# Transposing Q and K as bf16 halves, and centring K by the full-sequence mean, in a grouped-query attention kernel

## The chip, the cores and the metric

The kernel runs on one core of a Trainium2 chip. The metric is device time in microseconds. One run is one execution. The kernel before takes 653.99 us (median of 12 runs, 653.10 to 654.54). Executions agree within about 0.3%, so a difference of 1% is well outside the noise, and one of 0.2% needs several runs of both kernels side by side.

## The reference

Sixteen batches, 16 query heads that share 8 key/value heads two by two, 384 queries, 384 keys, head size 256, all in bf16:

```python
B, Hq, Hkv, Sq, Sk, D = 16, 16, 8, 384, 384, 256
# q, k, v: normal * 0.05, bf16
k = jnp.repeat(k, rep, axis=1); v = jnp.repeat(v, rep, axis=1)      # rep = 2
scores = jnp.einsum("bhqd,bhkd->bhqk", q, k) * D ** -0.5
p = softmax(scores, axis=-1)
return jnp.einsum("bhqk,bhkd->bhqd", p, v)
```

Entries of 0.05 make the scaled scores about 0.0025 in size, so every row of the softmax is almost flat and the output is nearly the mean of V. Comparing outputs on these inputs therefore hardly tests the scores at all.

## The kernel before

The work is 128 groups, one per batch and key/value head. A group has 768 query rows (two heads) and 384 keys. TensorE does three things per group: it transposes Q and K so that the head dimension lies on the partitions, it multiplies them (scores, transposed, keys on partitions), and it multiplies the exponentials with V (PV). One extra column of ones in V yields the row sums. The stages of neighbouring groups are interleaved in thirds of a slot, so that TensorE always has something to do.

The head size is 256, twice the partition count. The kernel before reads each pair of bf16 numbers as one f32 word, so one f32 transpose moves both:

```python
qT_sb  = ... sbuf_tensor("qT_sb",  [P, NBT, NQ], F32)     # bf16 pairs, interleaved
kT_sb  = ... sbuf_tensor("kT_sb",  [P, NBK, Sk], F32)
kcT_sb = ... sbuf_tensor("kcT_sb", [P, NBT, Sk], F32)
...
# TensorE, T(g, part): three row blocks
for s, (kind, t) in enumerate(parts[part]):
    src = (q_sb if kind == "q" else k_sb)[:, sl, t, :].bitcast(F32)
    i = pe.transpose(tr_ps[bank][:, s * P:(s + 1) * P], src, ident[:])     # ident is f32
```

What arrives is interleaved: partition p holds dimensions 2p and 2p+1 of token 0, then of token 1, and so on. The score matmul therefore picks every second element of both operands, even ones first, odd ones second, and adds the two products:

```python
# TensorE, ST(g, c)
for e in range(2):
    i = pe.matmul(st_ps[bank][:, 0:CW],                                    # CW = 384
                  lhsT=kcb[:, 2 * j * P + e:2 * (j + 1) * P:2],            # stationary, stride 2
                  rhs=qTb[:, 2 * h * CW + e:2 * (h + 1) * CW:2],           # moving, stride 2
                  start=(e == 0), stop=(e == 1))
```

`lhsT` is the stationary operand (128x128; the trace records a weight load for each matmul, 97 ns in the scores), `rhs` the moving one (128x384 in the scores; the wider it is, the further apart the matmuls start: 55.8 ns at 128 bf16 columns and 162.5 ns at 384 in the changed kernel). Before that, K is centred: a mean over keys is subtracted from each dimension, which leaves the softmax unchanged. VectorE sums the first 128 keys (`NMEAN = P`), and POOL subtracts:

```python
# VectorE, KRED(g)
kTb = kT_sb[:, slk, 0:NMEAN].bitcast(BF16).rearrange("p (k e) -> p e k", e=2)
i = dve.tensor_reduce(out=nsum_sb[:, slk, :], in_=kTb, axis=AX.X, op=ALU.add, negate=True)
# POOL, ksub(g): kc = NMEAN * k - sum, for e in 0, 1
i = pool.tensor_scalar(out=kcb[:, e::2], in0=kTb[:, e::2], scalar1=float(NMEAN),
                       scalar2=nsum_sb[:, slk, e:e + 1], op0=ALU.mult, op1=ALU.add)
```

ACT copies the transposes out of PSUM, the memory that TensorE writes to (EV), and computes the exponentials (EXP); VectorE divides by the row sums (NORM).

The softmax here doesn't subtract the row's maximum and nothing guards it: scores larger than these inputs give would overflow.

## Time and profile before

| | before |
|---|---|
| time, median | 653.99 us |
| TensorE busy | 99% of the span |
| ACT, VectorE, POOL busy | 74%, 73%, 27% |
| period of one group (PV starts 92 groups apart, divided by 92) | 5.000 us |

First the profile's page of the kernel before: the busy time of each engine, and the chain of work that ended last, by engine and by line. (PE is TensorE, PEld its weight loads, DVE is VectorE, ACT is ScalarE, POOL is GpSimd, and SPq the queue that issues the transfers.)

```profile
PE 643.8 (99%) x4992; PEld 499.0 (77%) x4992; DVE 472.5 (73%) x1664; ACT 483.4 (74%) x1153; POOL 173.4 (27%) x263
...
PE 98%; DMA 1%; DVE 1%; SPq 0%; issue 0%
PE ps L228 40%; PE ps L245 39%; PE ps L213 19%; DMA q_sb<-in_q_dram 1%; DVE o_sb L348 0%; DVE rs_sb L345 0%; SPq L141 0%; SPq L136 0%
```

TensorE is busy 99% of the time, and following each instruction back to what released it stays on TensorE for 98% of the span. Line 228 is the score matmul, 245 PV, 213 the transposes. The other engines have slack.

Busy time alone would not prove a bound, because the recorded durations of matmuls overlap. The groups of the page show it (the columns are line, engine, operation, output and inputs, sizes and count, then busy us and mean ns of one, then idle us before them):

```profile
L228 PE MATMUL ps<-qT_sb,kcT_sb 128*128 128x384 bf16 x1536 | 324.1, 332 | 0.0
L245 PE MATMUL ps<-v_sb,pT_sb 128*128 128x257 bf16 x2304 | 315.4, 272 | 0.2
L189 POOL TENSOR_SCALAR kcT_sb<-kT_sb,nsum_sb 128x384 bf16<-128x384 bf16 x256 | 172.6, 701 | 462.3 <-DVE nsum_sb L333 462.3
L304 ACT COPY qT_sb<-ps 128x384 f32<-128x384 f32 x256 | 122.6, 479 | 105.1 <-PE ps L213 105.1
L213 PE MATMUL ps<-ident,q_sb 128*128 128x128 f32 x768 | 127.0, 275 | 1.0 <-DMA q_sb<-in_q_dram 0.9
L333 DVE TENSOR_REDUCE nsum_sb<-kT_sb 128x2 f32<-128x256 bf16 x128 | 53.8, 420 | 11.0 <-ACT kT_sb L304 10.1
```

1536 score matmuls of 332 ns each would be 510 us, yet they cover 324 us. The cost of a matmul is the distance from its start to the next start, so read the timeline. This is TensorE of the kernel before in a stretch of 1.8 us (start, length, engine, line, what, and how many are merged):

```profile
300.14 0.49 PE L213 MATMUL ps<-ident,q_sb 128*128 128x128 f32 x3
300.47 0.84 PE L228 MATMUL ps<-qT_sb,kcT_sb 128*128 128x384 bf16 x4
301.15 0.82 PE L245 MATMUL ps<-v_sb,pT_sb 128*128 128x257 bf16 x6
301.81 0.49 PE L213 MATMUL ps<-ident,q_sb 128*128 128x128 f32 x3
```

Subtract neighbouring starts: three transposes take 0.33 us, four score matmuls 0.68 us, six PV matmuls 0.66 us, then it repeats. Averaged over single starts between 100 and 600 us, the spacing is 109.2 ns for an f32 transpose, 170.4 ns for a score matmul and 109.6 ns for PV. A group has 9, 12 and 18 of them: 9 x 109.17 + 12 x 170.42 + 18 x 109.58 = 5000 ns, exactly the period. Nothing else is in it.

### The profile page before, as it was taken

The page shows a single profiled execution, that of the slowest core. Times are in us where ns is not written, and L with a number is a line of the kernel's source. Part 1 is how long each engine was busy: PE and PEld are TensorE (multiplying, and loading weights), DVE is VectorE, ACT ScalarE, POOL GpSimd, SP SyncE. Part 2 cuts the span into 40 slices and gives each one's busy share as a digit, 9 for nine tenths or more (in the row PEclk, how much of TensorE's full clock was granted, in tenths as well). Part 3 has the DMA queues.
Part 4 walks back from the last instruction along what each step waited for, and adds up shares of the span by engine and source line. Part 5 has one row for each costly group of instructions (what it writes and reads, how often), then busy time and mean ns, then how long its engine had stood idle before and what let it go on. Part 6 is the DMA issues. An engine that isn't in the chain of part 4 may idle for free.

```text
span 651.6 us, 15000 instructions
## 1 busy us (share of the span) xinstructions
PE 643.8 (99%) x4992; PEld 499.0 (77%) x4992; DVE 472.5 (73%) x1664; ACT 483.4 (74%) x1153; POOL 173.4 (27%) x263
## 2 busy tenths in 40 slices
PE   7999999999999999999999999999999999999997
PEld 5777777777777777777777777777777777777775
DVE  2777777777777777777777777777777777777777
ACT  6777777777777777777777777777777777777774
POOL 3222322232223222222222232223222322232220
PEclk9999999999999999999999999999999999999999
DMA  7677777777777777777777777877777777777763
GB/s 254 215 227 239 247 236 229 234 230 245 237 247 242 232 235 239 243 230 238 241 241 227 241 222 236 249 241 234 240 232 242 247 234 229 242 243 238 229 203 117
DMA packets 125291, 151.99 MB, mean 233 GB/s; under 512 B 10272, under 2 KB 108960, under 8 KB 125216
## 3 DMA queue, kind: packets, MB, share of 16 engines
q1 hardware_dynamic: 125216, 151.04, 73.3%
q8 instruction: 41, 0.67, 0.5%
q14 instruction: 34, 0.28, 0.1%
HBM read 100.66 MB, written 50.33 MB: 232 GB/s over the span
## 4 chain that ended last, share of the span: by engine, by line
PE 98%; DMA 1%; DVE 1%; SPq 0%; issue 0%
PE ps L228 40%; PE ps L245 39%; PE ps L213 19%; DMA q_sb<-in_q_dram 1%; DVE o_sb L348 0%; DVE rs_sb L345 0%; SPq L141 0%; SPq L136 0%
## 5 line engine op out<-in xcount | busy, mean ns | idle before, releaser
L348 DVE TENSOR_TENSOR o_sb<-ps,rs_sb 128x256 bf16<-128x256 f32 x768 | 325.7, 424 | 26.4
L282 ACT ACTIVATE pT_sb<-ps 128x384 bf16<-128x384 f32 x768 | 337.9, 498 | 2.5 <-PE ps L228 2.5
L228 PE MATMUL ps<-qT_sb,kcT_sb 128*128 128x384 bf16 x1536 | 324.1, 332 | 0.0
L245 PE MATMUL ps<-v_sb,pT_sb 128*128 128x257 bf16 x2304 | 315.4, 272 | 0.2
L189 POOL TENSOR_SCALAR kcT_sb<-kT_sb,nsum_sb 128x384 bf16<-128x384 bf16 x256 | 172.6, 701 | 462.3 <-DVE nsum_sb L333 462.3
L245 PEld LDWEIGHTS ps<-v_sb,pT_sb 128*128 128x128 bf16 x2304 | 222.2, 97 | 77.7 <-DVE o_sb L348 1.2
L345 DVE RECIPROCAL rs_sb<-ps 128x1 f32<-128x1 f32 x768 | 124.9, 163 | 139.5 <-PE ps L245 129.6
L304 ACT COPY qT_sb<-ps 128x384 f32<-128x384 f32 x256 | 122.6, 479 | 105.1 <-PE ps L213 105.1
L228 PEld LDWEIGHTS ps<-qT_sb,kcT_sb 128*128 128x128 bf16 x1536 | 149.4, 97 | 61.1 <-issue 0.3
L213 PE MATMUL ps<-ident,q_sb 128*128 128x128 f32 x768 | 127.0, 275 | 1.0 <-DMA q_sb<-in_q_dram 0.9
L304 ACT COPY kT_sb<-ps 128x384 f32<-128x384 f32 x128 | 61.2, 478 | 53.5 <-PE ps L213 53.5
L213 PEld LDWEIGHTS ps<-ident,q_sb 128*128 128x128 f32 x768 | 93.0, 143 | 5.1 <-DMA q_sb<-in_q_dram 1.3
L213 PE MATMUL ps<-ident,k_sb 128*128 128x128 f32 x384 | 63.6, 275 | 3.4 <-DMA k_sb<-in_k_dram 3.4
L333 DVE TENSOR_REDUCE nsum_sb<-kT_sb 128x2 f32<-128x256 bf16 x128 | 53.8, 420 | 11.0 <-ACT kT_sb L304 10.1
L213 PEld LDWEIGHTS ps<-ident,k_sb 128*128 128x128 f32 x384 | 46.5, 143 | 5.1 <-issue 3.4
L304 ACT ACT_TABLE_LOAD x1 | 1.3, 1283 | 0.8 <-PEq L381 0.8
L174 POOL TENSOR_SCALAR_AFFINE_SELECT ident<-ones_sb 128x128 f32<-128x128 f32 x1 | 0.3, 292 | 0.1
L171 POOL MEMSET ones_sb<- 128x128 f32 x1 | 0.2, 204 | 0.3 <-POOLq L381 0.3
L381 POOL MEMSET const-float32-0.0<- 128x1 f32 x1 | 0.1, 98 | 0.3 <-issue 0.3
L177 POOL MEMSET v_sb<- 128x9 bf16 x1 | 0.1, 136 | 0.0
L381 POOL MEMSET const-bfloat16-1.0<- 128x1 bf16 x1 | 0.1, 102 | 0.0
L381 POOL MEMSET const-uint8-127<- 128x1 uint8 x1 | 0.1, 102 | 0.0
(1 smaller groups left out, 0.1 us busy)
## 6 DMA issues: line engine op xcount, KB each, us to landing
q_sb<-in_q_dram SPq DMA_DIRECT2D x256, 192.0 KB, 3.6
out_dram<-o_sb SPq DMA_DIRECT2D x127, 384.0 KB, 3.1
k_sb<-in_k_dram SPq DMA_DIRECT2D x128, 192.0 KB, 3.4
v_sb<-in_v_dram SPq DMA_DIRECT2D x128, 192.0 KB, 3.7
out_dram<-o_sb SPq DMA_DIRECT2D x3, 128.0 KB, 1.7
```

Of the source, the lines that this page charges most:

```text
L171: i = pool.memset(ones_sb[:], 1.0)
L174: pool.affine_select(out=ident[:], in_=ones_sb[:], pattern=[[-1, P]], compare_op=ALU.is_equal, fill=0.0, base=0, channel_multiplier=1)
L189: i = pool.tensor_scalar(out=kcb[:, e::2], in0=kTb[:, e::2], scalar1=float(NMEAN), scalar2=nsum_sb[:, slk, e:e + 1], op0=ALU.mult, op1=ALU ...
L213: i = pe.transpose(tr_ps[bank][:, s * P:(s + 1) * P], src, ident[:])
L228: i = pe.matmul(st_ps[bank][:, 0:CW], lhsT=kcb[:, 2 * j * P + e:2 * (j + 1) * P:2], rhs=qTb[:, 2 * h * CW + e:2 * (h + 1) * CW:2], start=( ...
L245: i = pe.matmul(o_ps[bank][:, 0:D + 1], lhsT=pT_sb[:, slp, j, t * P:(t + 1) * P], rhs=v_sb[:, slv, j, 0:D + 1], start=(j == 0), stop=(j == ...
L282: i = act.activation(out=pT_sb[:, slp, j, h * CW:(h + 1) * CW], in_=st_ps[bank][:, 0:CW], func=ACTF.Exp, bias=-C0, scale=scale / NMEAN)
L304: i = act.copy(out=dst, in_=tr_ps[bank][:, 0:nb * P])
L333: i = dve.tensor_reduce(out=nsum_sb[:, slk, :], in_=kTb, axis=AX.X, op=ALU.add, negate=True)
L345: i = dve.reciprocal(rs_sb[:, ri:ri + 1], o_ps[bank][:, D:D + 1])
L348: i = dve.tensor_tensor(out=o_sb[:, so, t, :], in0=o_ps[bank][:, 0:D], in1=rs_sb[:, ri:ri + 1].broadcast_to([P, D]), op=ALU.mult)
L381: nc = _bacc.Bacc("TRN2", target_bir_lowering=False, num_devices=1)
```

## The change

The change has two intentions: to transpose bf16 as bf16, in two halves of 128 dimensions, so that every operand is contiguous; and to centre K by the mean over all 384 keys. The core of the diff (helper functions, semaphore allocation and a constant that cancels in the softmax are cut):

```diff
-    NMEAN = P
+    NMEAN = Sk
-        qT_sb = ... [P, NBT, NQ], F32        kT_sb, kcT_sb likewise, ident F32
+        qT_sb = ... [P, NBT, 2, NQ], BF16    kT_sb, kcT_sb likewise, ident BF16
+        ksum_sb = es.enter_context(nc.sbuf_tensor("ksum_sb", [P, NBK, 2, P], F32))
 # TensorE, transposes
-                    src = (q_sb if kind == "q" else k_sb)[:, sl, t, :].bitcast(F32)
-                    i = pe.transpose(tr_ps[bank][:, s * P:(s + 1) * P], src, ident[:])
+                    src = q_sb if kind == "q" else k_sb
+                    for m in range(2):
+                        blk = m * nb + s
+                        i = pe.transpose(trb[:, blk * P:(blk + 1) * P],
+                                         src[:, sl, t, m * P:(m + 1) * P], ident[:])
 # TensorE, scores
-                                  lhsT=kcb[:, 2 * j * P + e:2 * (j + 1) * P:2],
-                                  rhs=qTb[:, 2 * h * CW + e:2 * (h + 1) * CW:2],
+                                  lhsT=kcT_sb[:, sl, m, j * P:(j + 1) * P],
+                                  rhs=qT_sb[:, sl, m, h * CW:(h + 1) * CW],
 # POOL
+            def kfold(g):      # 384 keys folded to 128 by two adds, waits for K's copy
+                ...
             for i in slots:
+                if valid(i + 2):
+                    ksub(i + 2)
                 if valid(i + 3):
-                    ksub(i + 3)
+                    kfold(i + 3)
 # VectorE
-                    if u == 0 and valid(i + 3):
-                        KRED(i + 3)          # summed kT_sb, first 128 keys
+                if valid(i + 3):
+                    KRED(i + 3)              # sums ksum_sb, at the end of the slot
```

ACT still copies the same bytes out of PSUM as 384 f32 words. One part of the diff shown matters for the schedule: the subtraction for a group now runs one slot later than before (a slot is one period of the interleaved stages).

More of the change, by code (lines that the diff above doesn't have):

```diff
@@ L13, with __init__ @@
 class Sem:
-    def __init__(self, nc, name):
-        self.h = nc.alloc_semaphore(name)
+    def __init__(self, es, nc, name):
+        self.h = es.enter_context(nc.semaphore(name))
         self.count = 0
@@ L32, in wait, with _split3 @@
         self.waited[key] = val
+def _split3(n):
+    base, rem = divmod(n, 3)
+    out_, s0 = [], 0
+    for x in range(3):
+        sz = base + (1 if x < rem else 0)
+        out_.append(list(range(s0, s0 + sz)))
+        s0 += sz
+    return out_
 def bass_standalone__gqa_softmax__near_ridge_kernel(nc, q, k, v, out):
@@ L42, in bass_standalone__gqa_softmax__near_ridge_kernel @@
     KT = Sk // P
-    DP = D // 2
-    assert DP == P and NQ % P == 0 and Sk % P == 0
+    assert D == 2 * P and NQ % P == 0 and Sk % P == 0 and Hq % Hkv == 0
     G = B * Hkv
     scale = float(D) ** -0.5
-    C0 = 50.0
+    C0 = 64.0
     VW = D + 8
-    CW = max(w for w in range(P, 513, P) if NQ % w == 0 and (NQ // w) * KT >= 1)
+    CW = max(w for w in range(P, 513, P) if NQ % w == 0)
     NCQ = NQ // CW
@@ L70, in bass_standalone__gqa_softmax__near_ridge_kernel @@
         v_sb = es.enter_context(nc.sbuf_tensor("v_sb", [P, NBV, KT, VW], BF16))
-        qT_sb = es.enter_context(nc.sbuf_tensor("qT_sb", [P, NBT, NQ], F32))
-        kT_sb = es.enter_context(nc.sbuf_tensor("kT_sb", [P, NBK, Sk], F32))
-        kcT_sb = es.enter_context(nc.sbuf_tensor("kcT_sb", [P, NBT, Sk], F32))
+        qT_sb = es.enter_context(nc.sbuf_tensor("qT_sb", [P, NBT, 2, NQ], BF16))
+        kT_sb = es.enter_context(nc.sbuf_tensor("kT_sb", [P, NBK, 2, Sk], BF16))
+        kcT_sb = es.enter_context(nc.sbuf_tensor("kcT_sb", [P, NBT, 2, Sk], BF16))
         pT_sb = es.enter_context(nc.sbuf_tensor("pT_sb", [P, NBP, KT, NQ], BF16))
         o_sb = es.enter_context(nc.sbuf_tensor("o_sb", [P, NBO, QT, D], BF16))
-        ident = es.enter_context(nc.sbuf_tensor("ident", [P, P], F32))
+        ident = es.enter_context(nc.sbuf_tensor("ident", [P, P], BF16))
         ones_sb = es.enter_context(nc.sbuf_tensor("ones_sb", [P, P], F32))
         nsum_sb = es.enter_context(nc.sbuf_tensor("nsum_sb", [P, NBK, 2], F32))
+        ksum_sb = es.enter_context(nc.sbuf_tensor("ksum_sb", [P, NBK, 2, P], F32))
         rs_sb = es.enter_context(nc.sbuf_tensor("rs_sb", [P, 16], F32))
         ps = es.enter_context(nc.psum_tensor("ps", [P, 8, 512], F32))
+        s_lk = [Sem(es, nc, f"lk{i}") for i in range(NBQ)]
+        s_lq = [[Sem(es, nc, f"lq{i}_{pp}") for pp in range(NPT)] for i in range(NBQ)]
+        s_lv = [Sem(es, nc, f"lv{i}") for i in range(NBV)]
+        s_so = [Sem(es, nc, f"so{i}") for i in range(NBO)]
+        s_tr = Sem(es, nc, "tr")
+        s_st = Sem(es, nc, "st")
+        s_pv = Sem(es, nc, "pv")
+        s_ex = Sem(es, nc, "ex")
+        s_ev = Sem(es, nc, "ev")
+        s_rc = Sem(es, nc, "rc")
+        s_nm = Sem(es, nc, "nm")
+        s_ns = Sem(es, nc, "ns")
+        s_cn = Sem(es, nc, "cn")
+        s_init = Sem(es, nc, "init")
+        s_pl = Sem(es, nc, "pl")
+        s_ks = Sem(es, nc, "ks")
         block = es.enter_context(nc.Block())
@@ L85, in bass_standalone__gqa_softmax__near_ridge_kernel @@
         o_ps = [ps[:, TRB + STB + b, :] for b in range(OB)]
-        s_lk = [Sem(nc, f"lk{i}") for i in range(NBQ)]
-        s_lq = [[Sem(nc, f"lq{i}_{pp}") for pp in range(NPT)] for i in range(NBQ)]
-        s_lv = [Sem(nc, f"lv{i}") for i in range(NBV)]
-        s_so = [Sem(nc, f"so{i}") for i in range(NBO)]
-        s_tr = Sem(nc, "tr")
-        s_st = Sem(nc, "st")
-        s_pv = Sem(nc, "pv")
-        s_ex = Sem(nc, "ex")
-        s_ev = Sem(nc, "ev")
-        s_rc = Sem(nc, "rc")
-        s_nm = Sem(nc, "nm")
-        s_ns = Sem(nc, "ns")
-        s_cn = Sem(nc, "cn")
-        s_init = Sem(nc, "init")
-        s_pl = Sem(nc, "pl")
         def grp(g):
@@ L128, in valid @@
             return 0 <= g < G
+        cs, ts, psl = _split3(NCH), _split3(QT), _split3(NPT)
         @block.sync
@@ L140, in load_qk @@
                     nb = len(parts[part])
-                    s_lq[sl][part].inc(sp.dma_start(q_sb[:, sl, t0:t0 + nb, :], qd[:, t0:t0 + nb, :]), 16)
+                    s_lq[sl][part].inc(
+                        sp.dma_start(q_sb[:, sl, t0:t0 + nb, :], qd[:, t0:t0 + nb, :]), 16)
             def load_v(g):
@@ L154, in store @@
                     s_nm.wait(sp, QT * g + t0 + step)
-                    s_so[so].inc(sp.dma_start(od[:, t0:t0 + step, :], o_sb[:, so, t0:t0 + step, :]), 16)
+                    s_so[so].inc(
+                        sp.dma_start(od[:, t0:t0 + step, :], o_sb[:, so, t0:t0 + step, :]), 16)
                 so_done_target[g] = s_so[so].count
@@ L178, in _ @@
             s_init.inc(i)
+            def kfold(g):
+                slk = g % NBK
+                s_ev.wait(pool, NPT * g + 1)
+                if g >= NBK:
+                    s_ns.wait(pool, g - NBK + 1)
+                if KT == 1:
+                    i = pool.tensor_copy(ksum_sb[:, slk], kT_sb[:, slk, :, 0:P])
+                else:
+                    i = pool.tensor_tensor(out=ksum_sb[:, slk], in0=kT_sb[:, slk, :, 0:P],
+                                           in1=kT_sb[:, slk, :, P:2 * P], op=ALU.add)
+                    for j in range(2, KT):
+                        s_pl.inc(i)
+                        s_pl.wait(pool, s_pl.count)
+                        i = pool.tensor_tensor(out=ksum_sb[:, slk], in0=ksum_sb[:, slk],
+                                               in1=kT_sb[:, slk, :, j * P:(j + 1) * P], op=ALU.add)
+                s_ks.inc(i)
             def ksub(g):
@@ L185, in ksub @@
                     s_st.wait(pool, NCH * (g - NBT + 1))
-                kTb = kT_sb[:, slk, :].bitcast(BF16)
-                kcb = kcT_sb[:, sl, :].bitcast(BF16)
-                for e in range(2):
-                    i = pool.tensor_scalar(out=kcb[:, e::2], in0=kTb[:, e::2],
-                                           scalar1=float(NMEAN), scalar2=nsum_sb[:, slk, e:e + 1],
+                for m in range(2):
+                    i = pool.tensor_scalar(out=kcT_sb[:, sl, m, :], in0=kT_sb[:, slk, m, :],
+                                           scalar1=float(NMEAN), scalar2=nsum_sb[:, slk, m:m + 1],
                                            op0=ALU.mult, op1=ALU.add)
@@ L210, in T @@
                     s_ev.wait(pe, n - TRB + 1)
+                nb = len(parts[part])
+                trb = tr_ps[bank].bitcast(BF16)
                 for s, (kind, t) in enumerate(parts[part]):
-                    src = (q_sb if kind == "q" else k_sb)[:, sl, t, :].bitcast(F32)
-                    i = pe.transpose(tr_ps[bank][:, s * P:(s + 1) * P], src, ident[:])
+                    src = q_sb if kind == "q" else k_sb
+                    for m in range(2):
+                        blk = m * nb + s
+                        i = pe.transpose(trb[:, blk * P:(blk + 1) * P],
+                                         src[:, sl, t, m * P:(m + 1) * P], ident[:])
                 s_tr.inc(i)
@@ L224, in ST @@
                     s_ex.wait(pe, n - STB + 1)
-                qTb = qT_sb[:, sl, :].bitcast(BF16)
-                kcb = kcT_sb[:, sl, :].bitcast(BF16)
-                for e in range(2):
+                for m in range(2):
                     i = pe.matmul(st_ps[bank][:, 0:CW],
-                                  lhsT=kcb[:, 2 * j * P + e:2 * (j + 1) * P:2],
-                                  rhs=qTb[:, 2 * h * CW + e:2 * (h + 1) * CW:2],
-                                  start=(e == 0), stop=(e == 1))
+                                  lhsT=kcT_sb[:, sl, m, j * P:(j + 1) * P],
+                                  rhs=qT_sb[:, sl, m, h * CW:(h + 1) * CW],
+                                  start=(m == 0), stop=(m == 1))
                 s_st.inc(i)
@@ L249, in PV @@
                 s_pv.inc(i)
-            def split3(n):
-                base, rem = divmod(n, 3)
-                sizes = [base + (1 if x < rem else 0) for x in range(3)]
-                out_, s0 = [], 0
-                for sz in sizes:
-                    out_.append(list(range(s0, s0 + sz)))
-                    s0 += sz
-                return out_
-            cs, ts, psl = split3(NCH), split3(QT), split3(NPT)
             for i in slots:
@@ L293, in EV @@
                 kind, t0 = blocks[0]
+                H = P // 2
                 if kind == "q":
@@ L297, in EV @@
                         s_st.wait(act, NCH * (g - NBT + 1))
-                    dst = qT_sb[:, sl, t0 * P:(t0 + nb) * P]
+                    dst = qT_sb[:, sl].bitcast(F32)[:, :, t0 * H:(t0 + nb) * H]
                 else:
@@ L302, in EV @@
                         s_cn.wait(act, g - NBK + 1)
-                    dst = kT_sb[:, sl, t0 * P:(t0 + nb) * P]
-                i = act.copy(out=dst, in_=tr_ps[bank][:, 0:nb * P])
+                    dst = kT_sb[:, sl].bitcast(F32)[:, :, t0 * H:(t0 + nb) * H]
+                src = tr_ps[bank][:, 0:2 * nb * H].rearrange("p (m x) -> p m x", m=2)
+                i = act.copy(out=dst, in_=src)
                 s_ev.inc(i)
-            def split3(n):
-                base, rem = divmod(n, 3)
-                sizes = [base + (1 if x < rem else 0) for x in range(3)]
-                out_, s0 = [], 0
-                for sz in sizes:
-                    out_.append(list(range(s0, s0 + sz)))
-                    s0 += sz
-                return out_
-            cs, psl = split3(NCH), split3(NPT)
             for i in slots:
@@ L328, in KRED @@
                 slk = g % NBK
-                s_ev.wait(dve, NPT * g + 1)
+                s_ks.wait(dve, g + 1)
                 if g >= NBK:
                     s_cn.wait(dve, g - NBK + 1)
-                kTb = kT_sb[:, slk, 0:NMEAN].bitcast(BF16).rearrange("p (k e) -> p e k", e=2)
-                i = dve.tensor_reduce(out=nsum_sb[:, slk, :], in_=kTb, axis=AX.X, op=ALU.add,
-                                      negate=True)
+                i = dve.tensor_reduce(out=nsum_sb[:, slk, :], in_=ksum_sb[:, slk],
+                                      axis=AX.X, op=ALU.add, negate=True)
                 s_ns.inc(i)
@@ L350, in NORM @@
                 s_nm.inc(i)
-            def split3(n):
-                base, rem = divmod(n, 3)
-                sizes = [base + (1 if x < rem else 0) for x in range(3)]
-                out_, s0 = [], 0
-                for sz in sizes:
-                    out_.append(list(range(s0, s0 + sz)))
-                    s0 += sz
-                return out_
-            ts = split3(QT)
             for i in slots:
```

## The prediction

It was written from the kernel, the diff and the profile of before, without running the change. The 162.5 ns that it expects of a contiguous score matmul and the 55.8 ns of a bf16 transpose are not shown by any trace of before; the changed kernel's trace shows them, 162.50 and 55.83 ns.

> **What bounds the kernel now.** TensorE. The summary of busy time has PE at 643.8 of 651.6 us (99%); the chain of waits is 98% PE (L228 scores 40%, L245 PV 39%, L213 transposes 19%); the list of waits shows under 10 us of PE idle, nearly all at the start and end. The other engines hold 73% (DVE), 74% (ACT), 27% (POOL). The granted clock is full. So only the spacing of TensorE's instructions counts.
>
> From the starts of single matmuls in the trace, a group of heads takes 5.0 us (128 groups), three equal thirds of 1.667 us:
> - 4 score matmuls, 384 columns, stride-2 operands: 169 to 173 ns apart, 682 ns together;
> - 6 PV matmuls, 257 columns, unit stride: 110 ns apart, 658 ns;
> - 3 f32 transposes: 109 ns apart, 328 ns.
>
> [...] The score matmul should take 162.5 but takes 170.5: about 8 ns too much, and what distinguishes it is the stride of two on both operands.
>
> **What changes on TensorE.**
> 1. Transposes: 3 f32 become 6 bf16[...] 55.8 ns each, so 335 ns for 328: +7 ns per third, about +3 us in all. The f32 version was already paying only twice a bf16 pass, so halving the element doubles the count and saves nothing. Risks: twice the weight loads with short matmuls to hide them behind. The trace bounds this: where a weight load came late (at 645.7 us) the next matmul started 120 instead of 110 ns later, so an exposed bf16 load costs about 11 ns; and where the sequencer had run dry, instructions start 31 ns apart, so a pair needs about 62 ns. So 56 to 67 ns per transpose: +3 to +28 us, I think near the low end[...].
> 2. Scores: operands become unit stride. If the stride costs the 8 ns, 12 matmuls x 128 groups x 8 ns = -12 us. I give this 65%.
> 3. PV is untouched.
>
> **What changes elsewhere, off the critical path.** POOL gains two tensor-tensor adds per group; from 701 ns for its 384-element operation I estimate 1.2 to 2 us more, POOL then near 3 of 5 us. VectorE's reduction still reads 256 elements (420 ns, about the same) and moves to the end of the slot. ACT copies still move 384 f32 words (479 ns). The chain transpose, evacuate, fold, reduce, subtract gets longer, and the subtraction moves one slot later, but must be done only by the next slot: I estimate 2 us of slack left. Prologue: at most 1 us more. DMA bytes are unchanged.
>
> **Predicted time.** 654.2 + 4 (transposes) - 10 (scores, weighted) = 648 us; 642 to 666 should hold it 8 times in 10. Faster by over 2%: 0.10; within 2%: 0.78; slower by over 2%: 0.12.
>
> **What would show each step.** Score matmuls 163 ns apart instead of 170 (right) or still 170 (stride innocent; total near 657). Transposes 56 ns apart, 335 ns per six; if 62 to 67, the load or the sequencer is exposed. TensorE still about 99% busy; no new waits of PE on POOL's centred K. ACT copy still about 480 ns, VectorE reduction about 420 ns, POOL busy near double.
>
> **What would make it wrong.** Transposes at 80 ns or more apart (+25 ns x 18 x 128 = +58 us: slower); the fold on POOL so slow, or so blocked by VectorE, that scores wait for centred K; the stride costing nothing.

## The result and the profile after

The changed kernel takes 645.18 us (median of 8 runs, 644.34 to 646.14), beside 653.99 us for the kernel before. The ratio is 0.9866, with a 95% interval of 0.9856 to 0.9876. Ratios here are the mean time of one kernel's fast runs over that of the other's of the same rounds, so not quite the ratio of the medians quoted.

The page of the changed kernel, engines and chain (line 264 is now the score matmul, 281 PV, 250 the transposes):

```profile
PE 635.0 (99%) x6144; PEld 505.4 (79%) x6144; DVE 460.6 (72%) x1664; ACT 483.6 (75%) x1153; POOL 320.0 (50%) x519
...
PE 98%; DMA 1%; DVE 1%; SPq 0%; issue 0%
PE ps L281 39%; PE ps L264 39%; PE ps L250 20%; DMA q_sb<-in_q_dram 1%; DVE o_sb L367 0%; DVE rs_sb L364 0%; SPq L156 0%; SPq L150 0%
```

TensorE is still the bound, at 99%. POOL has nearly doubled, from 173 to 320 us, and the list of waits shows no wait of TensorE on it. The groups that answer to those shown of before:

```profile
L281 PE MATMUL ps<-v_sb,pT_sb 128*128 128x257 bf16 x2304 | 316.3, 273 | 0.2
L264 PE MATMUL ps<-qT_sb,kcT_sb 128*128 128x384 bf16 x1536 | 312.7, 326 | 0.0
L220 POOL TENSOR_SCALAR kcT_sb<-kT_sb,nsum_sb 128x384 bf16<-128x384 bf16 x256 | 147.8, 589 | 280.9 <-DVE nsum_sb L352 280.9
L333 ACT COPY qT_sb<-ps 128x384 f32<-128x384 f32 x256 | 122.8, 480 | 99.2 <-PE ps L250 99.2
L250 PE MATMUL ps<-ident,q_sb 128*128 128x128 bf16 x1536 | 128.6, 220 | 0.8 <-DMA q_sb<-in_q_dram 0.8
L204 POOL TENSOR_TENSOR ksum_sb<-kT_sb 128x256 f32<-128x256 bf16 x128 | 85.7, 669 | 19.2 <-ACT kT_sb L333 3.4
L209 POOL TENSOR_TENSOR ksum_sb<-ksum_sb,kT_sb 128x256 f32<-128x256 f32 x128 | 85.9, 671 | 10.0
L352 DVE TENSOR_REDUCE nsum_sb<-ksum_sb 128x2 f32<-128x256 f32 x128 | 52.3, 409 | 11.6 <-POOL ksum_sb L209 11.6
```

The score matmuls cover 312.7 us where they covered 324.1. There are twice as many transposes, and they cover 128.6 us (Q) where they covered 127.0. POOL's two adds are new, 669 and 671 ns each. The same stretch of TensorE's timeline:

```profile
300.14 0.82 PE L281 MATMUL ps<-v_sb,pT_sb 128*128 128x257 bf16 x6
300.80 0.50 PE L250 MATMUL ps<-ident,q_sb 128*128 128x128 bf16 x6
301.14 0.81 PE L264 MATMUL ps<-qT_sb,kcT_sb 128*128 128x384 bf16 x4
301.79 0.60 PE L281 MATMUL ps<-v_sb,pT_sb 128*128 128x257 bf16 x4
```

Six transposes take 0.34 us (0.33 for three before) and four score matmuls 0.65 us (0.68 before). In single starts between 100 and 600 us:

| spacing, ns | before | after | per group | change per group |
|---|---|---|---|---|
| score matmul | 170.42 | 162.50 | 12 and 12 | -95 ns |
| transpose | 109.17 | 55.83 | 9 and 18 | +22 ns |
| PV | 109.58 | 110.00 | 18 and 18 | +8 ns |
| period | 5000 | 4935 | | -65 ns |

Over 128 groups that is -12.2 + 2.9 + 1.0 = -8.3 us. The time fell by 8.8 us; the rest is in the start-up, where the first PV matmul came at 12.3 instead of 12.8 us. That moment lies anywhere between 12.0 and 13.8 us in the traces of the two kernels and of variants that leave TensorE's start-up alone, so I put no meaning on it. The traces show where most of the scatter comes from: in the first microseconds TensorE runs at half rate (bf16 transposes 107 ns apart, contiguous scores 320 ns, where 55.8 and 162.5 ns follow), until the trace's first record of the full clock, and that record begins anywhere between 8.5 and 11.4 us in these traces (9.6 before, 8.7 after). The later it begins, the later the first PV, with one exception among the nine.

### The profile page after: what moved, and what is told of

It is laid out like the page before. It is cut to its first block, busy times and chain, and to the rows that moved or that the text cites. A ratio compares the mean times of both kernels' runs of the same rounds, so it can differ in the third digit from the quotient of the medians.

```text
span 642.8 us, 17560 instructions
## 1 busy us (share of the span) xinstructions
PE 635.0 (99%) x6144; PEld 505.4 (79%) x6144; DVE 460.6 (72%) x1664; ACT 483.6 (75%) x1153; POOL 320.0 (50%) x519
## 4 chain that ended last, share of the span: by engine, by line
PE 98%; DMA 1%; DVE 1%; SPq 0%; issue 0%
PE ps L281 39%; PE ps L264 39%; PE ps L250 20%; DMA q_sb<-in_q_dram 1%; DVE o_sb L367 0%; DVE rs_sb L364 0%; SPq L156 0%; SPq L150 0%
## 5 line engine op out<-in xcount | busy, mean ns | idle before, releaser
L264 PE MATMUL ps<-qT_sb,kcT_sb 128*128 128x384 bf16 x1536 | 312.7, 326 | 0.0
L220 POOL TENSOR_SCALAR kcT_sb<-kT_sb,nsum_sb 128x384 bf16<-128x384 bf16 x256 | 147.8, 589 | 280.9 <-DVE nsum_sb L352 280.9
L264 PEld LDWEIGHTS ps<-qT_sb,kcT_sb 128*128 128x128 bf16 x1536 | 134.4, 98 | 50.1 <-ACT pT_sb L309 0.3
L250 PE MATMUL ps<-ident,q_sb 128*128 128x128 bf16 x1536 | 128.6, 220 | 0.8 <-DMA q_sb<-in_q_dram 0.8
L250 PEld LDWEIGHTS ps<-ident,q_sb 128*128 128x128 bf16 x1536 | 108.0, 98 | 7.7 <-DMA q_sb<-in_q_dram 1.1
L204 POOL TENSOR_TENSOR ksum_sb<-kT_sb 128x256 f32<-128x256 bf16 x128 | 85.7, 669 | 19.2 <-ACT kT_sb L333 3.4
L209 POOL TENSOR_TENSOR ksum_sb<-ksum_sb,kT_sb 128x256 f32<-128x256 f32 x128 | 85.9, 671 | 10.0
L250 PE MATMUL ps<-ident,k_sb 128*128 128x128 bf16 x768 | 64.4, 220 | 3.4 <-DMA k_sb<-in_k_dram 3.4
L352 DVE TENSOR_REDUCE nsum_sb<-ksum_sb 128x2 f32<-128x256 f32 x128 | 52.3, 409 | 11.6 <-POOL ksum_sb L209 11.6
L250 PEld LDWEIGHTS ps<-ident,k_sb 128*128 128x128 bf16 x768 | 54.0, 98 | 6.6 <-issue 3.4
```

The source lines that it names most:

```text
L204: i = pool.tensor_tensor(out=ksum_sb[:, slk], in0=kT_sb[:, slk, :, 0:P], in1=kT_sb[:, slk, :, P:2 * P], op=ALU.add)
L209: i = pool.tensor_tensor(out=ksum_sb[:, slk], in0=ksum_sb[:, slk], in1=kT_sb[:, slk, :, j * P:(j + 1) * P], op=ALU.add)
L220: i = pool.tensor_scalar(out=kcT_sb[:, sl, m, :], in0=kT_sb[:, slk, m, :], scalar1=float(NMEAN), scalar2=nsum_sb[:, slk, m:m + 1], op0=ALU ...
L250: i = pe.transpose(trb[:, blk * P:(blk + 1) * P], src[:, sl, t, m * P:(m + 1) * P], ident[:])
L264: i = pe.matmul(st_ps[bank][:, 0:CW], lhsT=kcT_sb[:, sl, m, j * P:(j + 1) * P], rhs=qT_sb[:, sl, m, h * CW:(h + 1) * CW], start=(m == 0), ...
L352: i = dve.tensor_reduce(out=nsum_sb[:, slk, :], in_=ksum_sb[:, slk], axis=AX.X, op=ALU.add, negate=True)
```

## The experiments

**What had to be told apart.** The trace says that the score matmuls got cheaper. It does not say why: the change made both of their operands contiguous, replaced the f32 transposes beside them, and moved the centring, all at once. Theory M: the stride of the moving operand cost the 8 ns. Rival W: the stride of the stationary operand, through the weight load. Rival F: the f32 transposes in the same stream. For the rest: does the new centring cost or save anything, and where does its slack end?

**A warning on correctness.** Several kernels below are wrong; they read the right number of elements at the wrong places. To test the versions meant to be right, I executed the programs in software with Q and K 28 times larger. The relative error against a f32 computation was 0.0034 to 0.0035 for the kernel before, the changed kernel and three versions below (stationary operand strided, old centring, f32 transposes with de-interleaving), and 1.37 to 1.40 for two of the wrong ones (three of the sixteen batches compared).

### Only the stationary operand strided (right result)

```diff
-    out=kcT_sb[:, sl, m, :]
+    out=kcT_sb[:, sl, :, :].rearrange("p m s -> p (m s)")[:, m::2]                       # POOL writes interleaved
-    lhsT=kcT_sb[:, sl, m, j * P:(j + 1) * P]
+    lhsT=kcT_sb[:, sl, :, :].rearrange("p m s -> p (m s)")[:, 2*j*P + m:2*(j+1)*P:2]
```

> The changed kernel, but centred K is stored interleaved again, so only the stationary operand of the score matmul (the weight load) has stride two; the result stays right. Theory M (the moving operand's stride costs the 7.5 ns): score matmuls stay 163 ns apart, time 645 us. Rival W (the weight load's stride costs it): 170 ns apart, 645.2 + 1536 x 7.5 ns = 656.7 us. Rival F (neither: the f32 transposes in the same stream slow the score matmuls): 163 ns, 645 us.

Measured: 645.17 us (4 runs; ratio to before 0.9868, interval 0.9853 to 0.9883), score matmuls 162.5 ns apart. This is the changed kernel's time (645.18), closer than the noise of either. A weight load of the scores takes 98 ns in both traces. The stationary operand's stride of two costs nothing here; rival W falls.

### Only the moving operand strided (wrong result)

```diff
-    rhs=qT_sb[:, sl, m, h * CW:(h + 1) * CW]
+    rhs=qT_sb[:, sl, :, :].rearrange("p m s -> p (m s)")[:, 2*h*CW + m:2*(h+1)*CW:2]
```

> The changed kernel, but the score matmul reads Q with stride two over the same bytes (wrong result on purpose, same work); only the moving operand is strided. Theory M: 169 to 173 ns apart, 645.2 + 11.5 = 656.7 us. Rival W: 163 ns, 645 us. Rival F: 163 ns, 645 us. If both operands share the cost: in between.

Measured: 656.10 us (4 runs; ratio to before 1.0038, interval 1.0022 to 1.0055), score matmuls 170.2 ns apart. One operand, and the whole 8 ns is back. The line of the score matmul in the groups of the two kernels, the stationary operand strided first, the moving one second:

```profile
L264 PE MATMUL ps<-qT_sb,kcT_sb 128*128 128x384 bf16 x1536 | 313.0, 327 | 0.0
```
```profile
L264 PE MATMUL ps<-qT_sb,kcT_sb 128*128 128x384 bf16 x1536 | 324.3, 333 | 0.0
```

313.0 against 324.3 us for the same 1536 matmuls; 11.3 us apart, and the times are 10.9 us apart. Theory M stands.

### The two halves of the change, each alone (both wrong results on purpose)

The transposes alone: both edits above together, so bf16 transposes with strided scores (and the new centring, which is tested by itself below).

> Both operands of the score matmul strided, with the bf16 transposes kept (wrong result on purpose). This is the transpose part of the change alone. All but rival F: score matmuls 170 ns apart, time 654.0 (before) + 384 x 7 ns = 656.7 us, within 1 us. Rival F: 163 ns, 645 us.

Measured: 656.05 us (ratio 1.0038, interval 1.0023 to 1.0053), score matmuls 170.2 ns apart, transposes 55.8 ns.

The stride alone: the kernel before, reading its interleaved operands as if they were contiguous.

```diff
-    lhsT=kcb[:, 2 * j * P + e:2 * (j + 1) * P:2]
+    lhsT=kcb[:, e * Sk + j * P:e * Sk + (j + 1) * P]
-    rhs=qTb[:, 2 * h * CW + e:2 * (h + 1) * CW:2]
+    rhs=qTb[:, e * NQ + h * CW:e * NQ + (h + 1) * CW]
```

> The kernel before with its f32 transposes, but the score matmul reads both operands with unit stride (wrong result on purpose). This is the stride part of the change alone. Stride theories M or W: score matmuls 163 ns apart, 654.0 - 11.5 = 642.5 us, faster than the changed kernel by 2.7 us because three f32 transposes take 328 ns where six bf16 ones take 335. Rival F: still 170 ns, 654 us.

Measured: 642.57 us (ratio 0.9831, interval 0.9817 to 0.9846), score matmuls 162.5 ns apart with the f32 transposes still beside them. Rival F falls. The four kernels make a square:

| us | f32 transposes | bf16 transposes |
|---|---|---|
| scores strided | 653.9 (before, same job) | 656.05 |
| scores contiguous | 642.57 | 645.18 (changed) |

The changed kernel's time is from the first job; the other three are of one job, in which the version with only the stationary operand strided took 645.17. Down a column is the stride: -11.3 and -10.9 us. Along a row are the transposes, together with the new centring, which costs nothing that can be seen (below): +2.2 and +2.6 us. The bf16 transposes by themselves made the kernel slower; the change is faster because they leave the operands contiguous.

### How the stride's cost grows

The moving operand at stride four, in the changed kernel (wrong result):

```diff
-    rhs=qT_sb[:, sl, m, h * CW:(h + 1) * CW]
+    rhs=qT_sb[:, sl, :, :].rearrange("p m s -> p (m s)")[:, m:2 * NQ:4]
```

> The changed kernel with the moving operand of the score matmul at stride four (8 bytes; wrong result on purpose). If the cost of the moving stride is a fixed start-up per matmul: 170 ns as at stride two. If it grows with the bytes spanned: 177 ns or more, time 645.2 + 1536 x 14 ns = 667 us. If the moving stride is innocent: 163 ns.

Measured: 916.14 us (one run), score matmuls up to 340 ns apart. No expectation came near it. TensorE in its timeline:

```profile
300.51 1.52 PE L264 MATMUL ps<-qT_sb,kcT_sb 128*128 128x384 bf16 x4
301.85 0.62 PE L281 MATMUL ps<-v_sb,pT_sb 128*128 128x257 bf16 x4
```

Four matmuls took 1.34 us, where they took 0.65 us contiguous. So stride two costs 5% (170.2 ns for 162.5) and stride four halves the rate (340 ns). The cost is neither a fixed start-up nor linear in the bytes spanned.

The start-up of the same trace adds something, since TensorE runs at half rate there until about 10 us:

```profile
8.01 1.54 PE L264 MATMUL ps<-qT_sb,kcT_sb 128*128 128x384 bf16 x4
9.37 0.81 PE L250 MATMUL ps<-ident,k_sb 128*128 128x128 bf16 x6
9.99 1.54 PE L264 MATMUL ps<-qT_sb,kcT_sb 128*128 128x384 bf16 x4
11.35 0.52 PE L250 MATMUL ps<-ident,q_sb 128*128 128x128 bf16 x6
11.70 1.52 PE L264 MATMUL ps<-qT_sb,kcT_sb 128*128 128x384 bf16 x4
13.04 0.35 PE L250 MATMUL ps<-ident,q_sb 128*128 128x128 bf16 x3
```

Six transposes take 0.62 us early (9.37 to 9.99) and 0.35 us later, but four scores at stride four take 1.36 us early (8.01 to 9.37) and 1.34 us later: 340 ns each at either rate. At stride two, the version with only the moving operand strided has 319, 321 and 326 ns at half rate, where contiguous scores have 320. So at stride four the time does not follow TensorE's rate, and at stride two little of the 8 ns is left at half rate. What sets the 340 ns no run here isolates.

The other way, the kernel before with chunks of 256 columns (`CW = 256`), operands at stride two:

> The kernel before with score matmuls of 256 columns in place of 384 (nine chunks per group for six), operands still at stride two. One size changed: unit-stride spacing would be [...] 109.2 ns. If the stride costs a fixed start per matmul: 116.7 ns. If it costs in proportion to the columns (7.5 x 256/384 = 5 ns): 114.2 ns. The total is of no interest: 128 x 9 x 2 matmuls at about 115 ns for 128 x 12 at 170 ns, near 658 us if ACT keeps up with its nine exponentials.

Measured: 654.27 us (one run), score matmuls 113.6 ns apart. For a contiguous matmul of 256 columns I estimate 109.2 ns, halfway between the changed kernel's 55.83 ns for 128 columns and 162.50 ns for 384 (PV with its 257 takes 109.6; no contiguous score matmul of 256 columns was run). So the excess is 113.6 - 109.2 = 4.4 ns for 256 columns and 7.9 ns for 384: nearer to proportional (5.3 by columns) than to a fixed cost (7.9), and below both.

### The centring

Centring as before, over the first 128 keys, without POOL's fold (right result):

```diff
-    NMEAN = Sk
+    NMEAN = P
-                if valid(i + 3):
-                    kfold(i + 3)
 # VectorE waits for K's copy and sums kT_sb[:, slk, :, 0:P] itself
```

> The changed kernel with the old centring: mean over the first 128 keys, no fold on POOL. The centring part of the change is off the critical path in my theory: POOL busy falls from 320 to about 150 us and the time stays 645 us within 0.5 us. Rival: the longer chain on POOL and VectorE costs something: 644 us or less.

Measured: 644.99 us (4 runs; ratio 0.9862, interval 0.9847 to 0.9878), POOL busy 148 us instead of 320. The full-sequence mean costs nothing beyond the noise. To see how much room is left, the fold was repeated (the result stays right, as the fold is computed anew each time).

Twice:

> The fold done twice. With three folds a group took 795.4 / 128 = 6.2 us, bound by the ring fold, reduce, subtract; one fold less is 1.5 us less, 4.7 us, just under TensorE's 4.93 us. So 645 us, unchanged, if the ring is the whole cost; over 650 us if POOL's load reaches TensorE before its ring is the longer one.

Measured: 648.01 us (one run), 3 us over what I expected. The period of a group is 4.935 us, the changed kernel's to the nanosecond. The extra time is all in the start-up: the PV matmuls of group 8 begin at 55.3 us instead of 51.7. There the first groups go through the longer ring (fold, reduction, subtraction, next fold) without earlier groups to hide it, and I had counted the steady state only. But the waits of TensorE that the trace puts down to it are two, 0.8 us for centred K and 0.6 us for the normalisation. The rest of the 3.5 us goes with TensorE's half rate, which lasts until 13.5 us here and 8.7 us in the changed kernel; whether the wait prolonged it or chance did, one run doesn't say.

Three times:

> The changed kernel with POOL's fold done three times. POOL work per group of heads is then 3 x 1.5 + 1.16 = 5.7 us against a period of 4.93 us, so POOL must become the bound: 128 x 5.7 to 6.0 us = about 735 to 770 us, with TensorE waiting for centred K. This shows that the chain is live and where its slack ends. If it stays at 645 us the fold's durations in the trace are not real cost.

Measured: 797.13 us (one run), a period of 6.09 us. The ring through POOL is the bound, a little above my range, and the way it reaches TensorE is not the one I wrote. The waits of this kernel (engine and line, what it waited for, us in all, times, longest us):

```profile
DVE nsum_sb L362 <- POOL ksum_sb L219: 278.0, 128, 9.2
PEld ps L291 <- DVE o_sb L377: 161.7, 130, 2.8
PE ps L291 <- DVE o_sb L377: 125.3, 126, 2.6
```

TensorE hardly waits for centred K (3.5 us in all). It waits for VectorE's normalisation (line 291 is PV here, which needs a free PSUM bank). In VectorE's program the next normalisations come behind the reduction, and the reduction waits for POOL's fold: 278.0 us in all, up to 9.2 us at a time. TensorE's PV waits 125.3 us in all for the normalisations. So in this kernel the slow helper reaches the critical engine through the queue of a third one.

### A version that keeps the f32 transposes and still gets contiguous operands (right result)

The square says what the best corner is: f32 transposes and contiguous scores. To make it right, somebody must de-interleave. ACT can do so for Q while it copies out of PSUM, at the price of 768 bf16 elements for 384 f32 words; POOL does it for K as it subtracts. This is the changed kernel with:

```diff
 # TensorE: f32 transposes as in the kernel before, ident F32
 # ACT, Q parts
-    dst = qT_sb[:, sl].bitcast(F32)[:, :, t0 * H:(t0 + nb) * H]
-    src = tr_ps[bank][:, 0:2 * nb * H].rearrange("p (m x) -> p m x", m=2)
+    dst = qT_sb[:, sl, :, t0 * P:(t0 + nb) * P]
+    src = tr_ps[bank][:, 0:nb * P].bitcast(BF16).rearrange("p (x e) -> p e x", e=2)
 # ACT, K part: f32 copy, kT_sb stays interleaved
 # POOL, ksub
-    in0=kT_sb[:, slk, m, :]
+    in0=kT_sb[:, slk, :].bitcast(BF16)[:, m::2]
 # POOL, kfold: the same through a view "p (s e) -> p e s"
```

> A right version that may beat both: f32 transposes, with Q de-interleaved by ACT as it copies out of PSUM (768 bf16 elements for 384 f32 words) and K by POOL. TensorE alone would need 642.5 us. ACT's Q copies I estimate at [...]800 ns, so ACT goes from 1.25 to 1.57 us busy in two of three thirds of 1.64 us. If that fits: 642 to 643 us, 0.4% under the changed kernel. If ACT's lateness reaches TensorE (waits of score matmuls on the exponential): 646 us or more.

The first job gave 642.99 to 643.73 us in four executions, and 2379.96 us in the one that was profiled. In that one all three kinds of matmul are spaced wider by nearly the same factor, 3.8 to 3.9 (mostly 420 ns for a transpose, 630 for a score matmul, 421 for PV). The page's groups show it less evenly, as durations: PV (line 279) at 699 ns where it takes 273 in the changed kernel, and the score matmul (262) at 894 where it takes 326:

```profile
L279 PE MATMUL ps<-v_sb,pT_sb 128*128 128x257 bf16 x2304 | 1059.3, 699 | 0.0
L262 PE MATMUL ps<-qT_sb,kcT_sb 128*128 128x384 bf16 x1536 | 1052.7, 894 | 0.0
```

That is near a quarter of the usual rate, for the whole execution. (The record's clock of 1.0 for it is no evidence: this trace holds no clock record.) None of the nine other executions of this kernel shows it, so it is not what the kernel usually does; what caused it no run here tells. It is left out of all comparisons, and the kernel was taken again, beside the changed kernel.

> The first job's profiled execution of this kernel [...] (score matmuls 630 ns apart, 2380 us); the other four executions took 643.0 to 643.7 us. Taken again, beside the changed kernel, for a usable profile: 643 us, score matmuls 163 ns apart, f32 transposes 109 ns apart, ACT's Q copy about 800 ns, ACT's busy time up by about 80 us, TensorE still 99% busy.

> The changed kernel in the same job as the version above, so that the two can be compared: 645.2 us, ratio to before 0.9866.

Measured: 643.24 us (5 runs, 643.17 to 643.67; ratio 0.9837, interval 0.9824 to 0.9851) beside 644.82 us for the changed kernel (4 runs, 644.39 to 645.42; ratio 0.9862, interval 0.9848 to 0.9875). The intervals against the kernel before just touch, but the runs of the two, on one chip and in one job, do not overlap: 1.6 us, a quarter of a per cent. The page of that run, the engines and then two groups, ACT's copy of Q and the f32 transposes of Q:

```profile
PE 633.8 (99%) x4992; PEld 503.5 (78%) x4992; DVE 460.9 (72%) x1664; ACT 565.5 (88%) x1153; POOL 334.4 (52%) x519
...
L332 ACT COPY qT_sb<-ps 128x768 bf16<-128x768 bf16 x256 | 204.5, 799 | 57.3 <-PE ps L248 49.6
L248 PE MATMUL ps<-ident,q_sb 128*128 128x128 f32 x768 | 127.0, 275 | 1.4 <-DMA q_sb<-in_q_dram 1.0
```

The period is 4.912 us against 4.935, 3 us over 128 groups. In the profiled execution 2.1 us of it went back in a later start (first PV at 14.3 us, 12.2 in the changed kernel of the same job). One wait of TensorE there, 0.34 us, is for ACT's longer copy; otherwise TensorE is at half rate until 11.9 us, 8.6 in the other trace, a moment that scatters without the longer copy too. ACT pays with 566 us busy instead of 484, 88% of the span: its copy grew from 480 ns for 384 elements to 799 ns for 768, 0.83 ns for each element more. That is a thin margin for a quarter of a per cent, and I would take it only if nothing else needed ACT.

## Why the prediction was right

- **The bound.** TensorE, before and after, as the chain of waits showed. Right, and the period is the plain sum of spacings in both kernels (5000 and 4935 ns).
- **The expected spacings.** The trace of before did not show the 55.8 and 162.5 ns that I expected; the changed kernel's does, 55.83 ns at 128 columns and 162.50 ns at 384, contiguous. The straight line through these two gives 109.6 ns at PV's 257 columns, where 109.6 to 110.0 is measured. The expectation served to show which matmul was too slow before anything was tried: 170.4 against 162.5. From the trace of before alone an estimate comes near: PV's 109.58 ns for 257 columns, scaled to 384, is 163.7, also below 170.4.
- **The transposes.** Predicted +7 ns per third (+3 us), with up to +28 us if weight loads or the sequencer showed. Measured +7.5 ns per third, +2.9 us by spacing, +2.2 and +2.6 us in time. The weight loads, one for each transpose, take 98 ns in the trace and the transposes start 55.83 ns apart, so the loads overlap the matmuls. An f32 transpose takes 109.2 ns, about as much as two bf16 ones (111.7).
- **The scores.** Predicted -12 us if the stride costs the excess, at 65%. Measured -12.2 us by spacing, -11.3 and -10.9 us in time. The profile of before could not tell the stride from other causes, so this was a bet, stated as one, and it came out. The prediction did not say which operand; the runs say the moving one alone.
- **Off the path.** ACT's copy 479 to 480 ns, VectorE's reduction 420 to 409 ns, as predicted. POOL works 2.5 us per group, not near 3: the adds take 669 and 671 ns, within the estimate, but the subtraction became faster, 701 to 589 ns, once its output was contiguous (697 ns with the output alone strided, in the first experiment; 589 with the input alone strided, in the last).
- **Slack of the longer chain.** Estimated at 2 us. The two lines below are of the changed kernel's timeline, first POOL, then TensorE. POOL's subtraction ends at 303.90 + 1.16 = 305.06 us. The first scores of this slot begin at 302.78, and those that need the subtraction one period of 4.935 later, at 307.7: 2.7 us of slack. The repeated folds don't test this figure, because another limit comes first: the ring of fold, reduction and subtraction. With three folds the ring is the period, 6.09 us; less two folds of 1.5 us (two adds each, 0.75 us from start to start) it is 3.1 us by estimate, which leaves 1.8 us of 4.935. One fold more fits, two don't, as measured.

```profile
303.90 1.16 POOL L220 TENSOR_SCALAR kcT_sb<-kT_sb,nsum_sb 128x384 bf16<-128x384 bf16 x2 [2.23 <-DVE nsum_sb L352]
```
```profile
302.78 0.81 PE L264 MATMUL ps<-qT_sb,kcT_sb 128*128 128x384 bf16 x4
```

- **The size of the total.** 648 predicted, 645.18 measured. The term that was off is "-10 (scores, weighted)". It was meant as -12 us times its chance; at the stated 65% it should have read -8, so the sum was not even consistent, and the truth was -12 by spacing. The +4 for the transposes was +2.2 to +2.9. A weighted mean of two outcomes is a figure that neither outcome produces: the honest forecast was "about 645 or about 657".

What stays open: why a moving operand at stride two costs 5% (170.2 against 162.5 ns, at a granted clock of 1.0), and why PV's spacing rises from 109.6 to 110.0 ns in every kernel with contiguous scores. No run here looks inside a matmul.

## What to carry to other kernels

When one engine is busy 99% of the time, list the spacing of its instructions by kind and hold each against what the spacings of the other kinds suggest for its size; the kind that is over is where the gain lies. Keep the moving operand of a matmul contiguous (the score matmuls here: 162.5 ns, at stride two 170.2, at stride four 340), and let the stationary one, or a side engine with slack, take the stride: at stride two, in this kernel, neither cost any time (645.17 us with K written and loaded strided, POOL's subtraction at 697 ns instead of 589, beside 645.18). And split a change that does two things before crediting either: here the part named first in the title cost 2 to 3 us, and its side effect on the layout earned 11.
